# Attention and gated feed-forward on one core: first transfers in another order, sinks' product with 64 weight columns, late values products reordered

## The chip, the cores and the metric

The kernel runs on one core of a Trainium2 chip. The core has five engines that run side by side: TensorE (PE, with its weight loads shown apart as PEld), VectorE (DVE), ScalarE (ACT), GpSimd (POOL) and SyncE (SP), which here only issues transfers. ACT issues a few transfers too. Each engine takes its instructions strictly in the order of its list and waits at an instruction until what it needs is there. The metric is the device time of one execution in microseconds (us); of several runs the median is given.

## The reference, cut to what matters

Attention with a window of 128 positions and a few sink positions that every row may see, for 4 batches of 8 heads, 768 positions and 64 dimensions per head; its output, with heads side by side as 512 columns, goes through a gated feed-forward layer.

```python
scores = scale * np.matmul(q, k.transpose(0, 1, 3, 2))
is_sink = pos[None, :] < int(n_sink)
rel = pos[:, None] - pos[None, :]
in_window = (rel >= 0) & (rel < int(window))
scores = np.where(is_sink | in_window, scores, -1000000000.0)
a = softmax(scores)
attn = np.matmul(a, v)                      # (4, 8, 768, 64)
x = attn.transpose(0, 2, 1, 3).reshape(3072, 512)
h = x @ w_in                                # (3072, 2048)
g = h * np.cos(h)
out = g @ w_out                             # (3072, 512)
```

## The kernel before

**Tiling.** Queries are worked in chunks of 256 rows (CB = 2 blocks of 128). The first four chunks are the first 256 rows of the four batches ("early" chunks, which have no sink columns of their own); then follow, batch by batch, two "late" chunks (rows 256 and 512). Two chunks make a pair of 512 columns for the feed-forward layer: `h_pair` (L476) and `out_pair` (L521) run 12 and 12 products of 512 columns per slice of 128 hidden units, in fp32r with operands split into a high and a low part. While the feed-forward of one pair runs on PE, the attention of the next pair is woven between its products.

**What sets the order.** A planner (`Plan.order`) simulates five engines with estimated durations and due times and gives one list of steps; each step appends its instructions to the list of one engine. The engines then keep to these lists. A step's function may issue more instructions than its planned duration says; the planner looks at the duration alone.

**Start.** `setup` runs before the planned steps. On ACT it issues the two limits `n_sink` and `window` (L235, L236) and the first two weight pieces `raw_70` and `raw_71` (L247, 512 KB each). SP begins with the planned loads of the first q pair (`xq`, L923, two transfers of 64 KB) and the first k pair (`xk`). The limits are spread over 128 partitions by a small product on PE (L266, `both`) and make the masks on DVE (L1538 to L1563). Between the masks DVE converts the 64-bit weights of `raw_70` and `raw_71` (three instructions each, L583, L589, L595). The first softmax instruction of DVE is L1046. Idle products (L1532) stand on PE's list between the first real ones. `xq` and `xk` are single buffers: SP's next load of q waits until PE has turned the last one (L931). Transfers share eight completion semaphores in turn, so a transfer also waits until the eighth before it has landed.

**Late chunks.** Per head, `values` (L1215) makes seven products into one bank `av`: the two blocks of 128 keys at the edge give one product of 128 columns each for the high (weights 128 columns wide: high and low values side by side) and low probabilities (64 weight columns), the middle block one of 256 columns each, and one of 256 columns is the sinks' product, whose weights are `x1r` (the sinks' values) and whose moving operand is `gt`. `gt` comes from `sink_cols` (L1105, L1107 on DVE: for four heads the eight sink columns of p, rounded and rest, side by side in `gc`), a transpose on PE (L1120) and a copy. `x1r` is made once per batch by `vs_part` (L1095, L1096, four times two instructions on DVE) from `yt`, which `load_batch_v` (L858) fills with eight small transfers on SP, also once per batch. The first batch's eight are on SP's list early, behind the third weight piece; those of the others come at 292, 404 and 516 us.

The order of the products in `values` before:

```python
seq = [wide_hi]
if o.sj:
    seq.append((o.av[:, o.sj[0] * P :], lhs, gt[:, : len(o.sj) * P]))
seq += [*narrow[:2], wide_lo, *narrow[2:]]
```

## Time and profile before

| | |
|---|---|
| median of 3 runs | 726.91 us (726.79 to 726.95) |
| profiled execution, first to last instruction | 725.6 us |
| PE busy | 708.8 us (98%) |
| PEld / DVE / ACT / POOL busy | 584.1 / 599.3 / 527.7 / 127.5 us |
| transfers | 77.13 MB, mean 106 GB/s |
| granted TensorE clock | 0.999 of full speed |

The profiled execution is given by its span, 725.6 us; what lies around the span brings it to the time of the runs, 1.3 us more. The page's busy shares are means over stages: until about 70 us the early attention runs with ACT and DVE nearly full and idle products on PE; from 70 to 700 us PE is busy almost without a gap; the last 26 us store the output and check the inputs' range. A row of the timeline reads: start, duration, engine, line, operation, output<-inputs, size, count, and in brackets the idle time before it with what ended it. SPq and ACTq rows are transfers being issued; the time is that of the issue, not of the landing.

### The profile page before, as it was taken

To read this page: it belongs to the slowest core of one execution; us is meant where nothing else is said; L and a number is where in the kernel's file an instruction comes from. 1 tells how busy PE (TensorE), PEld (TensorE's weight loads), DVE (VectorE), ACT (ScalarE), POOL (GpSimd) and SP (SyncE) were. 2 spreads that over 40 slices of the span, in tenths; PEclk is the share of its full clock that TensorE was granted. 3 is DMA by queue.
4 is the path that set the end of the run, shared out by engine and by line. 5 is a ranking of instruction groups with operands and counts; after the bars stand their busy time and mean duration, and the time that the engine had idled before them with its cause. 6 is when DMAs were issued, how large, how long until landed. Compare 5 with 4: busy or idle time off the path is not lost.

```text
span 725.6 us, 12986 instructions
## 1 busy us (share of the span) xinstructions
PE 708.8 (98%) x3674; PEld 584.1 (81%) x3674; DVE 599.3 (83%) x1849; ACT 527.7 (73%) x1344; POOL 127.5 (18%) x213
## 2 busy tenths in 40 slices
PE   7998999999999999999999999999999999999996
PEld 7766787888888888888888888888888888888884
DVE  6889998988988978988978988878989865667762
ACT  3896976788697697796686886776887766566642
POOL 1010000001223222232231222232123222100000
PEclk9999999999999999999999999999999999999999
DMA  5665555533256333355433254433254500375551
GB/s 144 182 186 153 158 162 162 141 65 68 68 118 146 73 62 57 72 119 124 93 60 59 56 131 103 118 61 64 43 139 99 119 18 12 97 210 148 164 137 64
DMA packets 236501, 77.13 MB, mean 106 GB/s; under 512 B 221060, under 2 KB 221060, under 8 KB 236420
## 3 DMA queue, kind: packets, MB, share of 16 engines
q1 hardware_dynamic: 236128, 75.15, 43.4%
q10 hardware_dynamic: 292, 1.05, 0.5%
q8 instruction: 32, 0.52, 0.3%
q14 instruction: 49, 0.40, 0.2%
HBM read 69.86 MB, written 6.29 MB: 105 GB/s over the span
## 4 chain that ended last, share of the span: by engine, by line
PE 81%; ACT 11%; DVE 4%; issue 2%; DMA 1%; SPq 0%; ACTq 0%; DVEq 0%
PE acc L521 32%; PE h L476 32%; PE av L1215 5%; PE s L1024 4%; ACT p L1055 3%; PE s L968 2%; PE av L1191 2%; PE tp L1136 2%; ACT p L1073 1%; PE tp L1146 1%; PE qk L931 1%; ACT L485 1%; PE idle L1532 1%; ACT L1055 1%; ACT early L390 1%
## 5 line engine op out<-in xcount | busy, mean ns | idle before, releaser
L521 PE MATMUL acc<-whi_out,ghi 128*128 128x512 f32 x384 | 161.8, 421 | 0.0
L476 PE MATMUL h<-xhi,whi_in 128*128 128x512 f32 x384 | 155.2, 404 | 0.0
L476 PE MATMUL h<-xlo,whi_in 128*128 128x512 f32 x384 | 150.9, 393 | 0.0
L521 PE MATMUL acc<-whi_out,glo 128*128 128x512 f32 x384 | 150.8, 393 | 0.0
L521 PE MATMUL acc<-wlo_out,ghi 128*128 128x512 f32 x384 | 150.1, 391 | 0.0
L476 PE MATMUL h<-xhi,wlo_in 128*128 128x512 f32 x384 | 150.0, 391 | 0.0
L1174 POOL TENSOR_SCALAR_AFFINE_SELECT ph<-ph 128x512 fp32r<-128x512 f32 x128 | 87.4, 683 | 230.3 <-DVE ph L1167 226.4
L485 ACT ACTIVATE r<-h 128x512 f32<-128x512 f32 x96 | 57.1, 598 | 48.6 <-PE h L476 46.0
L476 PEld LDWEIGHTS h<-xlo,whi_in 128*128 128x128 f32 x384 | 72.1, 188 | 16.3
L521 PEld LDWEIGHTS acc<-whi_out,glo 128*128 128x128 f32 x384 | 72.1, 188 | 16.2
L476 PEld LDWEIGHTS h<-xhi,whi_in 128*128 128x128 f32 x384 | 72.2, 188 | 12.0 <-DVE r L498 0.3
L476 PEld LDWEIGHTS h<-xhi,wlo_in 128*128 128x128 f32 x384 | 72.4, 189 | 11.2
L521 PEld LDWEIGHTS acc<-whi_out,ghi 128*128 128x128 f32 x384 | 72.8, 190 | 10.7
L521 PEld LDWEIGHTS acc<-wlo_out,ghi 128*128 128x128 f32 x384 | 72.7, 189 | 9.4
L1055 ACT ACTIVATE p<-p,st 128x136 f32<-128x136 f32 (+1 forms) x192 | 79.2, 416 | 0.3
L498 DVE SCALAR_TENSOR_TENSOR r<-r,h 128x512 f32<-128x512 f32 x96 | 64.6, 674 | 16.9 <-ACT r L491 16.1
L506 ACT CAST ghi<-r 128x512 fp32r<-128x512 f32 x96 | 59.5, 619 | 22.8 <-PE acc L521 15.7
L512 DVE TENSOR_TENSOR glo<-r,ghi 128x512 fp32r<-128x512 f32 x96 | 66.3, 691 | 7.1 <-ACT ghi L506 6.3
L1046 DVE CUSTOM_DVE_ANT_0 p<-s,mk 128x136 f32<-128x136 f32 (+1 forms) x192 | 59.8, 313 | 6.5 <-PE s L968 3.1
L984 ACT CAST l<-tq 64x256 fp32r<-64x256 f32 x64 | 25.8, 403 | 46.7 <-PE s L1024 46.4
L1032 DVE COPY_PREDICATED s<-mk,s 128x128 f32<-128x128 int32 x128 | 37.3, 291 | 24.6 <-PE s L1024 22.5
L1024 PEld LDWEIGHTS s<-r,l 128*128 128x128 f32 x256 | 46.5, 188 | 12.3 <-DVE ph L1167 1.5
(153 smaller groups left out, 1302.3 us busy)
## 6 DMA issues: line engine op xcount, KB each, us to landing
xk<-in_k_dram SPq DMA_DIRECT2D x256, 48.0 KB
raw<-in_moe_w_out_dram SPq DMA_DIRECT2D x16, 512.0 KB
wt<-in_moe_w_in_dram SPq DMA_DIRECT2D x32, 256.0 KB
raw<-in_moe_w_in_dram SPq DMA_DIRECT2D x14, 512.0 KB
v<-in_v_dram SPq DMA_DIRECT2D x64, 96.0 KB
raw<-in_v_dram SPq DMA_DIRECT2D x32, 192.0 KB
out_dram<-wt SPq DMA_DIRECT2D x22, 256.0 KB
wt<-in_moe_w_out_dram SPq DMA_DIRECT2D x20, 256.0 KB
```

Source lines behind the costliest of these rows:

```text
L476: nc.tensor.matmul(out=o.h, lhsT=w[:, c, fs], rhs=xx[:, c, :], start=(c == 0 and n == 0), stop=(c == NC - 1 and n == 2),)
L485: nc.scalar.activation(out=o.r, in_=o.h, func=AF.Sin, scale=0.5)
L498: nc.vector.scalar_tensor_tensor(out=o.r, in0=o.r, scalar=0.5, in1=o.h, op0=ALU.subtract, op1=ALU.mult)
L506: nc.scalar.copy(out=o.ghi, in_=o.r)
L512: e.tensor_tensor(out=o.glo, in0=o.r, in1=f32(o.ghi), op=ALU.subtract)
L521: nc.tensor.matmul(out=y.acc[j], lhsT=gg[:, j * P : (j + 1) * P], rhs=w[:, f, :], start=(f == 0 and n == 0), stop=(f == NFT - 1 and n == 2),)
L1024: nc.tensor.matmul(out=o.s_ps[j][:, :w], lhsT=o.l[:, j * P : (j + 1) * P], rhs=r.rearrange("p n s -> p (n s)")[:, c0 : c0 + w], start=(n = ...
L1032: nc.vector.copy_predicated(out=o.s_ps[j][:, :P], mask=below.bitcast(I32), data=o.s_ps[j][:, SW : SW + P])
L1046: nc.vector.tensor_tensor_reduce(out=o.pj[j][:, :w], in0=o.s_ps[j][:, :w], in1=masks[min(o.i0 + j, 2)][:, :w], op0=ALU.add, op1=ALU.min, s ...
L1055: nc.scalar.activation(out=o.pj[j][:, :w], in_=o.pj[j][:, :w], func=AF.Exp, bias=o.lead.st[:, 0, o.nth, j : j + 1], scale=-1.0, accum_out= ...
L1174: nc.gpsimd.affine_select(out=ph[:, :, b, :], in_=f32(ph)[:, :, 1, :], pattern=[[0, 2 * CB], [(-1, 1)[b], P]], compare_op=(ALU.is_gt, ALU. ...
L1215: nc.tensor.matmul(out=dst, lhsT=lhs, rhs=rhs, start=(n == 0), stop=(n == len(seq) - 1), skip_group_check=True)
```

## The change

The change does four things.

1. **First transfers.** The planned steps for the first q and k loads no longer issue them; `setup` does, first of all: q on SP, k on ACT. The limits go to SP behind q, `raw_70` to ACT behind k, and `raw_71` to SP behind the limits.
2. **Sinks' values.** `load_batch_v` issues 16 small transfers per batch in place of 8 (each group of 8 sink rows four times). `vs_part` runs three instructions in place of two, on 32 partitions in place of 16: it rounds the values, multiplies by a column `odd16` that is -1 on every second group of 8 partitions and 0 else, and adds the values. High and low values so stand below each other on partitions and not side by side in columns. `x1r` has 512 columns to blank in place of 1024. `odd16` is made at the start by one POOL and two DVE instructions.
3. **Sink columns.** `sink_cols` writes the rounded part and the rest twice (32 elements per partition and instruction in place of 16), `gc` has 128 columns for each block in place of 112, its transpose and the copy to `gt` 128 partitions in place of 112. The sinks' product has 64 weight columns.
4. **Order of the products in `values`.** First block high and low, sinks, third block high and low, middle block low, middle block high.

```diff
-        nc.scalar.dma_start(out=nw_i[:, 0, :], in_=n_sink.unsqueeze(0))
-        nc.scalar.dma_start(out=nw_i[:, 1, :], in_=window.unsqueeze(0))
+        for e, load in zip((nc.sync, nc.scalar), env.boot):
+            load(e)
+        nc.sync.dma_start(out=nw_i[:, 0, :], in_=n_sink.unsqueeze(0))
+        nc.sync.dma_start(out=nw_i[:, 1, :], in_=window.unsqueeze(0))
...
+        nc.gpsimd.iota(odd16.bitcast(I32), pattern=[[0, 1]], base=0, channel_multiplier=1)
...
-        for raw, src in env.first:
-            nc.scalar.dma_start(out=raw.rearrange("p n w -> p (n w)"), in_=src)
+        for e, (raw, src) in zip((nc.scalar, nc.sync), env.first):
+            e.dma_start(out=raw.rearrange("p n w -> p (n w)"), in_=src)
...
-                    for dup in range(2):
+                    for dup in range(4):
...
+        def booting(load):
+            env.boot.append(load)
+
+            def fn(e):
+                pass
+            return fn
...
-                w = sink_values().rearrange("p (g a) b c d -> p g (a b) c d", g=2)
-                r = slice(h * 32, h * 32 + 2 * NSINK)
-                e.tensor_copy(out=w[r, :, h, 0, :], in_=o.vs32[r])
-                e.tensor_tensor(
-                    out=w[r, :, h, 1, :], in0=o.vs32[r], in1=f32(w)[r, :, h, 0, :], op=ALU.subtract
-                )
+                r = slice(h * 32, h * 32 + 32)
+                w = sink_values()[r, :, h // 2, h % 2, :]
+                e.tensor_copy(out=w, in_=o.vs32[r])
+                e.tensor_scalar(out=w, in0=f32(w), scalar1=odd16[r], scalar2=1.0, op0=ALU.mult, op1=ALU.mult)
+                e.tensor_tensor(out=w, in0=f32(w), in1=o.vs32[r], op=ALU.add)
...
+                        out=g5.bitcast(F32R)[:, :, h, :, 0],
+                        in_=oo.p[:, :, P:SW].unsqueeze(2).broadcast_to([P, CB, 2, NSINK]),
...
-                seq = [wide_hi]
-                if o.sj:
-                    lhs = sink_values()[:, o.pair, o.odd].rearrange("p a d -> p (a d)")
-                    seq.append((o.av[:, o.sj[0] * P :], lhs, gt[:, : len(o.sj) * P]))
-                seq += [*narrow[:2], wide_lo, *narrow[2:]]
+                sinks = o.av[:D], sink_values()[:, o.h // 4, o.pair % 2, o.odd], gt
+                seq = [
+                    block(0, o.phi, 2 * D), block(0, o.plo, D), sinks, block(2, o.phi, 2 * D),
+                    block(2, o.plo, D), block(1, o.plo, D), block(1, o.phi, 2 * D),
+                ]
...
-                    i = add(dma(2), load_natural(xq_t, src, CB), [bx], pq, lat=2.3 if g else 1.9)
+                    load = load_natural(xq_t, src, CB)
+                    i = add(dma(2), load if g else booting(load), [bx], pq, lat=2.3 if g else 1.9)
```

The planner's estimates are the same, and no step changes its place among the others. What changes on the lists is shown at three places.

SP's list from its first transfer, before (`xq` and `xk` are a pair's q and k, `vpe` and `v_76` values of the early chunks, `yt` the sinks' values of the first batch):

```order
L923 DMA xq<-in_q_dram 128x2x64 x2
L923 DMA xk<-in_k_dram 128x2x64 x2
L904 DMA vpe<-in_v_dram 128x2x64
L904 DMA v_76<-in_v_dram 128x2x64
L923 DMA xq<-in_q_dram 128x2x64 x2
L923 DMA xk<-in_k_dram 128x2x64 x2
L568 DMA raw_70<-in_moe_w_in_dram 128x1024
L858 DMA yt<-in_v_dram 8x2x64 x8
L923 DMA xq<-in_q_dram 128x2x64 x2
```

It was q, k, values, the second pair, the third weight piece, eight sink loads and then the third pair's q. The same place with the change:

```order
L930 DMA xq<-in_q_dram 128x2x64 x2
L236 DMA nw_i<-in_n_sink_dram 1x2
L237 DMA nw_i<-in_window_dram 1x2
L249 DMA raw_71<-in_moe_w_in_dram 128x1024
L911 DMA vpe<-in_v_dram 128x2x64
L911 DMA v_76<-in_v_dram 128x2x64
L930 DMA xq<-in_q_dram 128x2x64 x2
L930 DMA xk<-in_k_dram 128x2x64 x2
L575 DMA raw_70<-in_moe_w_in_dram 128x1024
L865 DMA yt<-in_v_dram 8x2x64 x16
L930 DMA xq<-in_q_dram 128x2x64 x2
```

The first k has left SP's list for ACT's, limits and `raw_71` have come to it, and the third pair's q stands behind 16 sink loads.

PE's list at one late head, the first of the second batch, before (`av` is the head's output bank, `ph` the probabilities, `vr` its values, `gt` and `x1r` the sinks):

```order
L1215 MATMUL av_2_0_3657<-ph_2_0_3588,vr_2_0_3524 128x256
L1215 MATMUL av_2_0_3657<-gt,x1r 128x256
L1215 MATMUL av_2_0_3657<-ph_2_0_3588,vr_2_0_3524 128x128
L1215 MATMUL av_2_0_3657<-ph_2_0_3588,vr_2_0_3524 64x128
L1215 MATMUL av_2_0_3657<-ph_2_0_3588,vr_2_0_3524 64x256
L1215 MATMUL av_2_0_3657<-ph_2_0_3588,vr_2_0_3524 128x128
L1215 MATMUL av_2_0_3657<-ph_2_0_3588,vr_2_0_3524 64x128
L521 MATMUL acc_0_2335<-whi_out,ghi_3566 128x512
```

The feed-forward product (L521) follows two products of 128 columns. With the change:

```order
L1228 MATMUL av_2_0_3684<-ph_2_0_3611,vr_2_0_3539 128x128
L1228 MATMUL av_2_0_3684<-ph_2_0_3611,vr_2_0_3539 64x128
L1228 MATMUL av_2_0_3684<-gt,x1r 64x256
L1228 MATMUL av_2_0_3684<-ph_2_0_3611,vr_2_0_3539 128x128
L1228 MATMUL av_2_0_3684<-ph_2_0_3611,vr_2_0_3539 64x128
L1228 MATMUL av_2_0_3684<-ph_2_0_3611,vr_2_0_3539 64x256
L1228 MATMUL av_2_0_3684<-ph_2_0_3611,vr_2_0_3539 128x256
L528 MATMUL acc_0_2350<-whi_out,ghi_3589 128x512
```

Now it follows the product of 256 columns; the sinks' product is third and not second. All 64 late heads have these two orders.

DVE's list where the first batch's sink values are made, before:

```order
L1095 CAST x1r<-yt 16x2x64
L1096 TENSOR_TENSOR x1r<-yt,x1r 16x2x64
L1095 CAST x1r<-yt 16x2x64
L1096 TENSOR_TENSOR x1r<-yt,x1r 16x2x64
L1095 CAST x1r<-yt 16x2x64
L1096 TENSOR_TENSOR x1r<-yt,x1r 16x2x64
L1095 CAST x1r<-yt 16x2x64
L1096 TENSOR_TENSOR x1r<-yt,x1r 16x2x64
```

These are four parts of two instructions each. With the change:

```order
L1109 CAST x1r<-yt 32x2x64
L1110 TENSOR_SCALAR x1r<-x1r,neg 32x2x64
L1111 TENSOR_TENSOR x1r<-x1r,yt 32x2x64
L1109 CAST x1r<-yt 32x2x64
L1110 TENSOR_SCALAR x1r<-x1r,neg 32x2x64
L1111 TENSOR_TENSOR x1r<-x1r,yt 32x2x64
```

Each of the four parts has one instruction more (two of the four are shown), on the same number of elements per partition.

## Rows read from the trace of the kernel before

**Rows 1.** The page: span, and busy time of each engine
```profile
span 725.6 us, 12986 instructions
PE 708.8 (98%) x3674; PEld 584.1 (81%) x3674; DVE 599.3 (83%) x1849; ACT 527.7 (73%) x1344; POOL 127.5 (18%) x213
```
**Rows 2.** Stretches: us, busy by engine (instructions), granted clock, transfers' share, GB/s
```profile
30.00:40.00 10.00, 9.12 (x56) 7.22 (x55) 9.14 (x34) 9.63 (x34) 0.00 (x0) 1.00 0.69 180
...
300.00:400.00 100.00, 99.69 (x541) 83.17 (x540) 85.85 (x280) 77.49 (x200) 27.30 (x45) 1.00 0.42 91
```
**Rows 3.** Timeline of PE around the values products of one late head
```profile
300.39 0.40 PE L521 MATMUL acc<-whi_out,glo 128*128 128x512 f32 x1
300.62 0.28 PE L1215 MATMUL av<-ph,vr 128*128 128x256 f32 x1
300.74 0.28 PE L1215 MATMUL av<-gt,x1r 128*128 128x256 f32 x1
300.87 0.53 PE L1215 MATMUL av<-ph,vr 128*128 128x128 f32 x5
301.23 0.45 PE L521 MATMUL acc<-whi_out,ghi 128*128 128x512 f32 x1
301.51 0.40 PE L521 MATMUL acc<-wlo_out,ghi 128*128 128x512 f32 x1
```
**Rows 4.** Timeline of the start, all engines
```profile
1.38 0.22 ACTq L236 DMA_DIRECT2D nw_i<-in_window_dram  x1
...
1.63 1.54 ACTq L247 DMA_DIRECT2D raw<-in_moe_w_in_dram  x2
...
2.96 0.16 DVE L265 CAST sm<-nw_i 1x4 f32<-1x4 int32 x1 [0.19 <-DMA nw_i<-in_window_dram]
...
4.47 0.16 DVE L269 COPY neg<-both 128x2 f32<-128x2 f32 x1 [1.35 <-PE both L266]
...
6.39 0.43 DVE L583 TENSOR_SCALAR wt<-raw 128x512 int32<-128x512 int32 x1 [0.72 <-DMA raw<-in_moe_w_in_dram]
...
7.69 0.66 PE L931 MATMUL qk<-ident,xk 128*128 128x128 f32 x2 [2.10 <-DMA xk<-in_k_dram]
...
9.83 0.34 SPq L568 DMA_DIRECT2D raw<-in_moe_w_in_dram  x1
...
10.27 3.74 SPq L858 DMA_DIRECT2D yt<-in_v_dram  x8
...
10.78 0.28 DVE L1046 CUSTOM_DVE_ANT_0 p<-s,mk 128x128 f32<-128x128 f32 x1
...
14.53 0.91 SPq L923 DMA_DIRECT2D xq<-in_q_dram  x2
...
18.54 0.38 PE L931 MATMUL qk<-ident,xq 128*128 128x128 f32 x2
...
20.02 0.37 ACT L390 COPY early<-qk 64x256 f32<-64x256 f32 x1 [3.30 <-PE qk L931]
```
**Rows 5.** Waits of SP's queue: line, releaser: us in total, times, longest
```profile
SPq L858 <- DMA raw<-in_moe_w_in_dram: 1.1, 1, 1.1
```
**Rows 6.** Timeline of DVE where the second batch's sink values are made
```profile
296.59 0.66 DVE L1095 CAST x1r<-yt 16x128 fp32r<-16x128 f32 x1
...
299.92 0.23 DVE L1095 CAST x1r<-yt 16x128 fp32r<-16x128 f32 x1
300.18 0.29 DVE L1096 TENSOR_TENSOR x1r<-yt,x1r 16x128 fp32r<-16x128 f32 x1
```
**Rows 7.** Timeline of DVE and PE at the first batch's sinks
```profile
187.50 0.29 DVE L1096 TENSOR_TENSOR x1r<-yt,x1r 16x128 fp32r<-16x128 f32 x1
...
188.75 0.28 PE L1215 MATMUL av<-gt,x1r 128*128 128x256 f32 x1
```
**Rows 8.** Stretches of 1 us at the start, columns as in rows 2
```profile
7.00:8.00 1.00, 0.31 (x2) 0.34 (x3) 0.90 (x5) 0.00 (x0) 0.00 (x0) 1.00 0.93 232
8.00:9.00 1.00, 1.00 (x6) 1.00 (x5) 0.97 (x5) 0.61 (x2) 0.00 (x0) 1.00 0.17 37
```

More of the change, by code (lines that the diff above doesn't have):

```diff
@@ L19 @@
 SW = P + NSINK
-GR = 96 + 2 * NSINK
 BW = 2 * P + NSINK
@@ L256, in setup @@
         nc.vector.tensor_copy(out=rc, in_=rc_i)
+        nc.vector.tensor_scalar(
+            out=odd16.bitcast(I32), in0=odd16.bitcast(I32), scalar1=4, scalar2=1,
+            op0=ALU.logical_shift_right, op1=ALU.bitwise_and,
+        )
+        nc.vector.tensor_single_scalar(out=odd16, in_=odd16.bitcast(I32), scalar=-1.0, op=ALU.mult)
         nc.vector.tensor_single_scalar(out=env.below, in_=rel, scalar=0.0, op=ALU.is_lt)
@@ L833, in x1r @@
                 env.x1r = ap.tile([P, NP * NT], F32R, name="x1r", tag="x1")
-                env.vs = env.x1r.rearrange("p (a b c d) -> p a b c d", a=NP, b=2, c=2)
+                env.vs = env.x1r[:, : NP * 2 * D].rearrange("p (g a o d) -> p g a o d", g=2, o=2, d=D)
             return env.x1r
@@ L922, in fn @@
                 for h in range(2):
-                    nc.sync.dma_start(out=dst[:, :, h, :], in_=src(h).rearrange("(n s) d -> s n d", s=P))
+                    e.dma_start(out=dst[:, :, h, :], in_=src(h).rearrange("(n s) d -> s n d", s=P))
+            return fn
[3 more added lines that the diff above has]
+                pass
             return fn
@@ L1117, in fn @@
             def fn(e):
-                o.gp = late_bank(o, 2)[:GR]
-                for n, j in enumerate(o.sj):
-                    nc.tensor.transpose(
-                        out=o.gp[:, n * P : (n + 1) * P], in_=gc[:, j], identity=ident,
-                    )
+                o.gp = late_bank(o, 2)
+                for j in range(CB):
+                    nc.tensor.transpose(out=o.gp[:, j * P : (j + 1) * P], in_=gc[:, j], identity=ident)
             return fn
@@ L1126, in fn @@
             def fn(e):
-                w = len(o.sj) * P
-                copy(e, gt[:GR, :w], o.gp[:, :w])
+                copy(e, gt, o.gp)
             return fn
@@ L1200, in fn, with block @@
                 o.av = late_bank(o, 1)
-                mms = {}
-                for t, w in ((o.phi, 2 * D), (o.plo, D)):
-                    for n, (kb, qs) in enumerate(o.cols):
-                        dst = o.av[:w, (qs[0] - o.i0) * P : (qs[-1] + 1 - o.i0) * P]
-                        lhs = o.vr[:, kb - o.kb0].rearrange("p a d -> p (a d)")[:, :w]
-                        mms.setdefault((w, len(qs)), []).append((dst, lhs, t[:, o.offs[n] * P : o.offs[n + 1] * P]))
-                (wide_hi,), (wide_lo,) = mms[2 * D, CB], mms[D, CB]
-                narrow = [m for pair in zip(mms[2 * D, 1], mms[D, 1]) for m in pair]
-                seq = [wide_hi]
-                if o.sj:
-                    lhs = sink_values()[:, o.pair, o.odd].rearrange("p a d -> p (a d)")
-                    seq.append((o.av[:, o.sj[0] * P :], lhs, gt[:, : len(o.sj) * P]))
-                seq += [*narrow[:2], wide_lo, *narrow[2:]]
+                def block(n, t, w):
+                    kb, qs = o.cols[n]
+                    return (
+                        o.av[:w, (qs[0] - o.i0) * P : (qs[-1] + 1 - o.i0) * P],
+                        o.vr[:, n].rearrange("p a d -> p (a d)")[:, :w], t[:, o.offs[n] * P : o.offs[n + 1] * P],
+                    )
+                sinks = o.av[:D], sink_values()[:, o.h // 4, o.pair % 2, o.odd], gt
[3 more added lines that the diff above has]
+                ]
                 for n, (dst, lhs, rhs) in enumerate(seq):
@@ L1237, in x_sum @@
             return fn
-        env.first = []
+        env.first, env.boot = [], []
         early = [buf("plo", 1), buf("vr", 1), buf("v32", C["XV"])]
@@ L1337, in before_softmax @@
                     pk = t - 7 * T + C["DQ"] + 1.2 if g else C["LD"] - 1
-                    i = add(dma(2), load_natural(xk_t, src, o.nkb), [bx], pk, lat=2.4 if g else 1.9)
+                    load = load_natural(xk_t, src, o.nkb)
+                    i = add(dma(2), load if g else booting(load), [bx], pk, lat=2.4 if g else 1.9)
                     i = add(
```

13 lines of the change are left out of this document (7 added, 6 removed).

## The prediction, made before the changed kernel was run

> **What bounds the kernel now.** I read the page first, then busy time by stretches, then the timelines of three places: a late head, the making of the sinks' values, and the start. The page shows PE busy for 708.8 of 725.6 us [rows 1]; the question is which stages make up the rest and what an edit is worth in each. Between 300 and 400 us PE is busy for 99.69 of 100 us, while DVE and ACT have room [rows 2]: there, whatever PE no longer does, and whatever it has to wait for, goes to the end almost in full. Between 30 and 40 us ACT is busy for 9.63 and DVE for 9.14 of 10 us [rows 2], and PE's share is high only because idle products stand on its list. Engines keep to their lists, so a delay that reaches ACT and DVE before 30 us is not worked off; it reaches the end too. The granted clock is 1.00 in these rows (2.4 GHz, the upper of its two levels), and nothing in the change empties PE for longer than before, so I leave it there. The profiled execution spans 725.6 us, the median run is 726.91; the 1.3 us between them I take over unchanged. So three sums are wanted: products' order (all late heads), start (once), sinks' values (once per batch).
>
> **Order of the products: -2.8 us.** PE's starts are the measure, since the ends of pipelined products overlap. A feed-forward product of 512 columns moves the next start on by 0.23 us (300.39 to 300.62) [rows 3]. The two of 256 columns take 0.12 and 0.13, the five that follow 0.36 together, that is four of 0.06 and one of 0.12. But the first feed-forward product after them takes 0.28 (301.23 to 301.51), 0.05 more than its kin [rows 3]. It is the one whose full weights (128 columns) must be loaded while a product of only 128 columns (0.06 us) runs; I read the 0.05 as the part of that load that stands out. After the change it follows a product of 256 columns, twice the cover, and 0.05 is less than the 0.06 that this adds. The seven products are the same in kind and columns (the sinks' weights are half as wide, which the steps do not show to matter: wide and narrow weights alike step by 0.06). 64 late heads times 0.05 is 3.2 us. About 0.3 us in 100 are idle on PE [rows 2], that is, in some places PE waits for others already, and there the gain only makes it wait longer; for this I take off 0.4. Bounds: 0 (the 0.05 is something else) and -3.3.
>
> The Trainium skill, page "TensorE: Matmul & The Clock Gate", section "The mechanism", says that a weight load overlaps running products only when it goes to another group of rows of the array. Taken alone that would put every load of 128 rows on the path and make the reorder worth nothing. The trace does not agree: weight loads and products together are busy for 584.1 + 708.8 us in a span of 725.6 [rows 1].
>
> **Start: +1.5 us.** What goes: PE waits 2.10 us for the first k until 7.69 [rows 4]. That wait ends earlier. But what is late next is on DVE: its first softmax instruction (10.78) stands behind its list of masks and weight pieces, and that list stood still for 0.72 us until `raw_70` had landed at 6.39 [rows 4]. From there to 10.78 are 4.39 us of list that do not shrink. So k alone is worth nothing unless `raw_70` is early; call d the shift of 6.39.
>
> The limits: the cast at 2.96 comes 1.58 us after the second limit's issue at 1.38 [rows 4]. Behind q's two issues (0.91 as at 14.53 [rows 4]) this is 3.9. Now 1.35 us of DVE's wait until 4.47 are for PE's small product behind warm-up products, so of the 0.9 I let a third remain (an estimate), and DVE reaches `raw_70`'s first instruction not at 6.39 - 0.72 = 5.67 but near 6.0. That gives d = -0.4 as the lower bound. `raw_70` itself: it is issued at about the time as before (two q-sized issues of k in place of the limits), k's 128 KB ahead of it. `raw_71`, though, no longer stands behind it on one queue but on SP's, in flight beside it. Transfers move 232 GB/s from 7 to 8 us and 37 from 8 to 9 [rows 8], so the first burst ends near 8.2; a weight piece (512 KB) takes 2.3 us alone at that rate. Served one after the other, `raw_70` lands about where it did, k's 0.57 us against the bytes of k and v that no longer mix with it: d near 0. Shared by halves, with `raw_71` issued 0.4 to 0.8 us behind (the limits' two issues, 0.22 or more each [rows 4]), `raw_70` lands that much before 8.3: d = 1.1 to 1.5. Landing together is the upper end, d = 1.9. I take 1.0, next to sharing.
>
> d goes on through SP: the third weight piece (9.83) needs `raw_70`'s buffer and moves by d [rows 4]. Behind it eight sink loads took 3.74 us, of which 1.1 were one wait for that piece to land [rows 4, 5]: (3.74 - 1.1) / 8 = 0.33 each. Sixteen take 2.65 more, so they end not at 14.01 but at 16.7 + d. The third pair's q, issued from 14.53 to 15.44, now goes from 16.7 + d; its second half is issued at 17.15 + d and needs 1.6 us (the limits' time) to 2.0, landing near 18.75 to 19.2 + d. PE turns it at 18.54, and ACT at 20.02 has already sat idle for 3.30 for PE's turns [rows 4], so ACT is moved by what PE is: +0.2 to +0.7, taken 0.5, plus d. Sum 1.5; bounds 0.1 (d = -0.4) and 2.4 (d = 1.9).
>
> **Sinks' values: +2.5 us.** Each part has one instruction more. In the second batch a part's first instruction takes 0.26 to the next (299.92 to 300.18) [rows 6]; the new one has the same 128 elements per partition, so four are 1.0 us on DVE, which runs these parts without a gap. One may be stretched as the first is (0.66 us [rows 6]): then 1.4. `sink_cols` has 16 elements more in each of eight instructions, too few for any row to price; up to 0.2. The last instruction now ends at 300.18 + 0.29 = 300.47 and the product that reads it starts at 300.74 [rows 3, 6]: of the 0.27 some 0.1 go to the weight load and the hand-over, so about 0.2 is slack and 0.8 becomes a wait of PE, behind which the whole feed-forward queues. Two of the narrow products now stand ahead of the sinks' in place of the wide one, 0.12 either way, so this does not move. Three batches of such a kind are 2.4. The first batch's last instruction ends at 187.50 + 0.29 = 187.79, its product starts at 188.75 [rows 7]: 0.96 of slack, 0.1 left. Together 2.5. Bounds 0.5 (DVE finds room ahead of the parts, as it is 85.85% busy there [rows 2]) and 3.9 (1.4 less 0.1 of slack, three times).
>
> At no cost: eight more loads per batch on SP later, 2.65 us, hidden behind the four heads that lie between their issue and their use (if not, the wait would show at the same product); 16 more partitions in the sinks' transposes and copies; two DVE and one POOL instruction at the start, which fall into the 1.35 and 0.72 that DVE waits there [rows 4].
>
> **Sum.** -2.8 + 1.5 + 2.5 = +1.2; 725.6 + 1.2 + 1.3 = 728.1 us. Its own range, with d from 0.2 to 1.5 and the sinks from 1.8 to 3.2, is 726.9 to 729.3.
>
> **Rivals.**
> B, faster: `raw_70` is on time and the sinks' values are covered. d = -0.4 gives 0.1 at the start, the sinks cost 0.5 and the order gives all of 3.2: -2.6, 724.3 us. For it: DVE has 14% of room in the late stages [rows 2]. Against: in the row where it counts the parts follow each other without a gap, 0.27 before their use [rows 3, 6].
> C, slower: the two weight pieces on two queues are served in turns and land together near 8.3. Then d = 1.9, the start costs 2.4, the sum is +2.1: 729.0 us. It decides from d = 1.25 on, since there the sum passes +1.45. For it: DVE waited for this very transfer, and the burst has no spare rate [rows 4, 8]. Against: `raw_70` is issued first and has a lead. The Trainium skill, page "DMA: Bandwidth & Descriptors", section "Queues, rings and completion order", says that each transfer engine goes round the queues that have work, a packet from each; that would be this rival. No row of before has two weight pieces on two queues.
> D, slower, the order does nothing: the 0.05 us after the values is not a weight load, but comes with the change from values to feed-forward, whatever the last columns are. Then 1.5 + 2.5 = +4.0: 730.9 us. For it: within the values 128-column products step by 0.06 with weights of 128 columns too, and nothing stands out there [rows 3]. Against: full loads hide wherever at least 256 columns run ahead of them, and only the cover is shorter here.
>
> **Chances.** Forecast 0.46, B 0.20, C 0.18, D 0.10, other 0.06. A measurement of this kernel can tell 0.2%, 1.45 us, from no change: 725.46 to 728.36 is "same". The forecast's own range puts 0.33 there and 0.13 above; B is faster; C and D are slower; of the rest 0.02, 0.03 and 0.01. So faster 0.22, same 0.36, slower 0.42. The range of 724.9 to 730.0 leaves out half of B, most of D and little else.
>
> **What would show it.** Right: DVE's L590, first on `raw_70`, later than 6.39 by about 1; SP's sink loads ending near 17.7 and the third pair's q turned by PE near 20.0; feed-forward products after the values stepping by 0.23; PE idle 0.8 us in the second, third and fourth batch before the first product that reads `x1r`. Wrong: L590 on time (B), the first product after the values still at 0.28 (D), or no wait before `x1r`'s reader. If the start's delay is there but ACT and DVE are caught up at 70 us, my claim that a delay of the early stage reaches the end is wrong.

## The result, and the profile after

The changed kernel takes 733.76 us (median of 4 runs, 733.05 to 734.57), the kernel before 726.93 on the same chip: a ratio of 1.0095, interval 1.0083 to 1.0107, or +6.9 us. The forecast was +1.2 (728.1, with a range to 730.0): right in sign, far off in size. The profiled execution is the shortest of the four, 733.05 us with a span of 731.3, so its own sum (5.7 us over [rows 1]) is 0.7 short of the median's, and 1.7 lie around it where 1.3 were taken over.

The page: span, and busy time of each engine.

```profile
span 731.3 us, 13064 instructions
PE 708.5 (97%) x3674; PEld 578.4 (79%) x3674; DVE 605.1 (83%) x1867; ACT 528.5 (72%) x1344; POOL 127.5 (17%) x214
```

PE is busy for as long as before [rows 1] and idle for longer. The same stretch in the middle of a batch in both shows it, first before, then after.

```profile
305.00:400.00 95.00, 94.69 (x513) 79.01 (x512) 81.03 (x267) 73.40 (x190) 26.30 (x43) 1.00 0.43 92
```

```profile
305.00:400.00 95.00, 93.81 (x509) 77.17 (x509) 81.75 (x269) 71.81 (x189) 25.97 (x43) 1.00 0.44 96
```

Granted clock 1.00 in both; PE's idle time has grown from 0.31 to 1.19 us in 95.

**Where it came in.** Each trace has the same 2304 products of 512 columns on PE. The start of the n-th in one trace less its start in the trace of before shows when a kernel falls behind (us; the head gives the time in the trace of before):

| kernel | 56 | 188 | 192 | 293 | 320 | 405 | 416 | 518 | 530 | 712 |
|---|---|---|---|---|---|---|---|---|---|---|
| changed | 2.86 | 2.40 | 3.23 | 3.10 | 4.24 | 4.00 | 5.27 | 5.04 | 6.28 | 6.18 |
| fused | 3.26 | 2.92 | 2.87 | 2.63 | 3.21 | 3.10 | 3.16 | 3.08 | 3.44 | 3.42 |
| order_only | 0.85 | 0.76 | 0.76 | 0.88 | 0.94 | 1.10 | 1.15 | 1.29 | 1.34 | 1.28 |
| before16 | 2.18 | 2.10 | 2.10 | 2.08 | 2.57 | 2.59 | 2.61 | 2.72 | 2.99 | 2.89 |
| before_gc | 0.49 | 0.07 | 0.02 | 0.29 | 0.31 | 0.53 | 0.59 | 0.76 | 0.83 | 1.12 |

The changed kernel is late after the start, falls back at the first head of each of the four batches (0.8, 1.1, 1.3 and 1.2 us), and in between wins back no more than 0.1 to 0.25 where the order should give 0.8 in 16 heads. Part of what is missing there is a drift of 0.2 to 0.3 us per batch that the wider sink columns alone show too (before_gc). Order_only has the start of before, unchanged, and yet 0.85 at 56: a single execution's start is known to no better than that. Taken together, and read in the same way for the other runs, the starts still part: three kernels with the start of before (order_only, before_gc, before_vpool) are 0.5 to 0.9 late at 56, four with sixteen loads and otherwise that start (before16, sinks_only, sinks_order, late_fused) 1.9 to 2.9. Fused had a granted clock of 0.50 from 21.0 to 24.4 us, so its start is not the change's alone.

**The start**, all engines, answering [rows 4] and [rows 5].

```profile
2.22 0.23 SPq L237 DMA_DIRECT2D nw_i<-in_window_dram  x1
...
5.50 0.16 DVE L272 CAST sm<-nw_i 1x4 f32<-1x4 int32 x1 [3.00 <-DMA nw_i<-in_window_dram]
...
7.45 0.42 DVE L590 TENSOR_SCALAR wt<-raw 128x512 int32<-128x512 int32 x1
...
11.32 6.52 SPq L865 DMA_DIRECT2D yt<-in_v_dram  x16
...
17.94 0.90 SPq L930 DMA_DIRECT2D xq<-in_q_dram  x2
...
20.49 0.41 PE L945 MATMUL qk<-ident,xq 128*128 128x128 f32 x2 [2.07 <-DMA xq<-in_q_dram]
...
22.00 0.37 ACT L397 COPY early<-qk 64x256 f32<-64x256 f32 x1 [5.55 <-PE qk L945]
```

The wait for k is gone (PE turns it at 7.25 without one). The limits, forecast for 3.9, are cast at 5.50, 3.3 us after their issue where it was 1.58: beside q, k and the weight pieces even eight bytes come late. `raw_70` is begun at 7.45 without a wait for it, so d (the shift of that first instruction on `raw_70`, before at 6.39) is 1.06, close to the 1.0 that was taken, but set by the limits. The sink loads end at 17.84, and PE turns the third pair's q at 20.49, 1.95 later than before.

**A late head**, PE, answering [rows 3].

```profile
303.79 0.39 PE L528 MATMUL acc<-whi_out,glo 128*128 128x512 f32 x1
304.02 0.28 PE L1228 MATMUL av<-ph,vr 128*128 128x128 f32 x2
304.14 0.28 PE L1228 MATMUL av<-gt,x1r 128*64 128x256 f32 x1
304.26 0.51 PE L1228 MATMUL av<-ph,vr 128*128 128x128 f32 x4
304.61 0.39 PE L528 MATMUL acc<-whi_out,ghi 128*128 128x512 f32 x1
304.84 0.39 PE L528 MATMUL acc<-wlo_out,ghi 128*128 128x512 f32 x1
305.07 0.40 PE L528 MATMUL acc<-whi_out,glo 128*128 128x512 f32 x1
306.09 0.41 PE L1149 MATMUL tp<-ident,p 128*128 128x128 f32 x2 [0.62 <-DVE st L1060]
```

The product after the values now steps by 0.23 (304.61 to 304.84): the 0.05 is saved, as forecast. But there is no wait before the product that reads `x1r`, where the forecast had it; PE waits 1.5 us later, at the transpose for a softmax that DVE is late with.

**The sinks' values of the second batch**, last part, DVE, answering [rows 6].

```profile
303.96 0.23 DVE L1109 CAST x1r<-yt 32x128 fp32r<-32x128 f32 x1
304.22 0.28 DVE L1110 TENSOR_SCALAR x1r<-x1r,neg 32x128 fp32r<-32x128 f32 x1
304.54 0.29 DVE L1111 TENSOR_TENSOR x1r<-x1r,yt 32x128 fp32r<-32x128 f32 x1
```

This part ends at 304.83, yet the sinks' product of the batch's first head began at 304.14: it needs its own part alone, the first, which had ended at 301.42.

### The profile page after: what moved, and what is told of

It reads as the page before. It is cut to its first block, busy times and chain, and to the rows that moved or that the text cites. A ratio compares the mean times of both kernels' runs of the same rounds, so it can differ in the third digit from the quotient of the medians.

```text
span 731.3 us, 13064 instructions
## 1 busy us (share of the span) xinstructions
PE 708.5 (97%) x3674; PEld 578.4 (79%) x3674; DVE 605.1 (83%) x1867; ACT 528.5 (72%) x1344; POOL 127.5 (17%) x214
## 4 chain that ended last, share of the span: by engine, by line
PE 71%; ACT 11%; DVE 10%; DMA 3%; issue 3%; SPq 1%; DVEq 0%; ACTq 0%
PE h L483 28%; PE acc L528 27%; PE av L1228 4%; PE s L1038 3%; ACT p L1069 3%; PE av L1204 2%; PE s L982 2%; PE tp L1149 2%; DMA xq<-in_q_dram 2%; ACT p L1087 1%; DVE glo L519 1%; PE tp L1159 1%; ACT L492 1%; PE qk L945 1%; ACT early L397 1%
## 5 line engine op out<-in xcount | busy, mean ns | idle before, releaser
L528 PE MATMUL acc<-whi_out,ghi 128*128 128x512 f32 x384 | 160.0, 417 | 0.0
```

The costliest lines, as they stand in the source:

```text
L528: nc.tensor.matmul(out=y.acc[j], lhsT=gg[:, j * P : (j + 1) * P], rhs=w[:, f, :], start=(f == 0 and n == 0), stop=(f == NFT - 1 and n == 2),)
```

## The experiments

Ratios are to the kernel before, timed beside each on the same chip. Microseconds are medians. Where a difference between two of these kernels is called good to so many us, that is half of its 95% interval, worked out from the two ratios.

**order_only.** The kernel before with the new order; sinks' weights stay 128 columns.

```diff
-                seq = [wide_hi]
-                if o.sj: ...
-                seq += [*narrow[:2], wide_lo, *narrow[2:]]
+                seq = [*narrow[:2], sinks, *narrow[2:], wide_lo, wide_hi]
```

> The kernel before with only the late values products in the new order (the sinks' product keeps 128 weight columns). Theory A (the gain is eaten): the step after the values falls from 0.28 to 0.23 us in all 64 heads, 3.3 us on PE, but PE then waits longer at the few places where it already waits for the softmax on DVE (0.3 to 0.4 us at 327, 375, 406 us and their like in each batch), so less than 1.5 us reach the end: 725.4 to 726.9 us. Theory B (the gain was lost only because the sinks' values slow DVE): alone the order gives 2.5 to 3.3 us, 723.6 to 724.4 us.

727.23 us, 1.0004 (0.9995 to 1.0013): no change. Neither theory had the reason. PE around the values:

```profile
301.50 0.28 PE L1213 MATMUL av<-ph,vr 128*128 128x128 f32 x2
301.62 0.33 PE L1213 MATMUL av<-gt,x1r 128*128 128x256 f32 x1
301.79 0.53 PE L1213 MATMUL av<-ph,vr 128*128 128x128 f32 x4
302.16 0.39 PE L521 MATMUL acc<-whi_out,ghi 128*128 128x512 f32 x1
302.39 0.40 PE L521 MATMUL acc<-wlo_out,ghi 128*128 128x512 f32 x1
```

The 0.05 has moved: the feed-forward product steps by 0.23, but the sinks' takes 0.17 (301.62 to 301.79) where it took 0.13 [rows 3]. Its full weights now stand behind a product of 128 columns. With 64 weight columns it steps by 0.12 in the changed kernel. So the order needs the narrow sinks' weights; the forecast had called their width indifferent.

**start_only.** The kernel before with the first transfers of the change alone.

```diff
+        for e, load in zip((nc.sync, nc.scalar), env.boot):
+            load(e)
+        nc.sync.dma_start(out=nw_i[:, 0, :], in_=n_sink.unsqueeze(0))
...
+        for e, (raw, src) in zip((nc.scalar, nc.sync), env.first):
```

> The kernel before with only the first transfers in the new order (eight sink loads per batch as before). Theory A (limits and sink loads both count): the limits are cast near 5.5 us and the first weight piece is begun near 7.45 as in the changed kernel, but the third pair's q is issued near 15.5 and not 17.9, so PE turns it at 18.6 to 19.3 us (18.54 before, 20.49 changed) and the end moves by +0.5 to +1.2: 727.4 to 728.1 us. Theory B (the late limits are all of it): +2.4 to +2.9, 729.3 to 729.8 us. Theory C (the sixteen loads are all of it): 726.6 to 727.2 us.

728.04 us, 1.0010 (1.0001 to 1.0019): theory A in its time, +0.7 to +1.0. Here DVE did wait for the weight piece:

```profile
7.18 0.43 DVE L585 TENSOR_SCALAR wt<-raw 128x512 int32<-128x512 int32 x1 [0.37 <-DMA raw<-in_moe_w_in_dram]
```

PE turned the third pair's q at 19.53, outside theory A's 18.6 to 19.3, but without a wait for it. In this execution PE had been idle for 1.93 us until 12.00, and the granted clock was 0.57 from 12 to 16 us; the ten others show a mean clock of 0.997 to 0.999 where this one has 0.995. So the 19.53 says nothing of when that q came.

**sinks_only.** The changed kernel with first transfers and order as before.

```diff
-        for e, load in zip((nc.sync, nc.scalar), env.boot):
-            load(e)
...
+                    block(1, o.phi, 2 * D), sinks, block(0, o.phi, 2 * D), block(0, o.plo, D),
+                    block(1, o.plo, D), block(2, o.phi, 2 * D), block(2, o.plo, D),
```

> The kernel before with only the sinks' part of the change: sixteen loads per batch, three DVE instructions per part, 64 weight columns; products and first transfers stand as before. Theory A (the third DVE instruction, once per batch, delays the softmax behind it and PE waits there): a jump of 0.8 to 1.1 us on PE at each of 189, 301, 413 and 525 us, together about 4, and from the sixteen loads at the start 0.3 to 1.2: 731.2 to 732.1 us. Theory B (the jumps came from PE arriving earlier through the new order, not from DVE): below 729.5 us.

734.41 us, 1.0103 (1.0088 to 1.0118), +7.5: more than the whole change, and more than theory A had. The sixteen loads of the start are in it, which the forecast had counted with the start.

**fused.** The changed kernel with two instructions per part:

```diff
-                e.tensor_scalar(out=w, in0=f32(w), scalar1=odd16[r], scalar2=1.0, op0=ALU.mult, op1=ALU.mult)
-                e.tensor_tensor(out=w, in0=f32(w), in1=o.vs32[r], op=ALU.add)
+                e.scalar_tensor_tensor(out=w, in0=f32(w), scalar=odd16[r], in1=o.vs32[r], op0=ALU.mult, op1=ALU.add)
```

> The changed kernel with multiplication and addition of the sinks' values in one DVE instruction: two per part, as before the change, all else as changed. Theory A (the number of DVE instructions makes the jumps): the jumps at 189, 301, 413 and 525 us fall from 0.85 to 1.1 to below 0.3 us each, the time by 3 to 4 us: 729.8 to 730.8 us. Theory B (wider sink columns, sixteen loads or the late order make them): 732.8 to 734.6 us, as the changed kernel.

730.22 us, 1.0044 (1.0030 to 1.0058), 3.7 below the changed kernel by the ratios (good to 1.3). Theory A in its time; the steps at the batches shrink to -0.05, 0.58, 0.06 and 0.36 (table), two of them not below the 0.3 that it had.

**limits_first.** The changed kernel with the limits back in front on ACT.

```diff
+        nc.scalar.dma_start(out=nw_i[:, 0, :], in_=n_sink.unsqueeze(0))
+        nc.scalar.dma_start(out=nw_i[:, 1, :], in_=window.unsqueeze(0))
         for e, load in zip((nc.sync, nc.scalar), env.boot):
             load(e)
-        nc.sync.dma_start(out=nw_i[:, 0, :], in_=n_sink.unsqueeze(0))
-        nc.sync.dma_start(out=nw_i[:, 1, :], in_=window.unsqueeze(0))
```

> The changed kernel with the two limits where they were, first on ACT's queue, k and the first weight piece behind them; SP's queue begins with q and the second weight piece. Theory A (limits behind q and beside k cast at 5.5 us move the masks, the first weight piece and the third by 1 us): the cast is back near 3.0 to 3.5 us, the third pair's q is turned about 1 us earlier than 20.49, and the time falls by 0.6 to 1.5 us from the changed kernel, 732.3 to 733.2 us. Theory B (the first weight piece, sharing with the second, sets the start, not the limits): 733.4 to 734.2 us, and DVE waits for the piece.

734.54 us, 1.0112 (1.0097 to 1.0127): not better, theory A fails in its number; DVE waits for the piece, as theory B had it. But this kernel changed more than meant, as its start shows.

```profile
1.82 0.46 SPq L249 DMA_DIRECT2D raw<-in_moe_w_in_dram  x1
...
2.60 0.49 ACTq L249 DMA_DIRECT2D raw<-in_moe_w_in_dram  x1
...
2.72 0.20 DVE L272 CAST sm<-nw_i 1x4 f32<-1x4 int32 x1 [0.21 <-DMA nw_i<-in_window_dram]
...
8.22 0.43 DVE L590 TENSOR_SCALAR wt<-raw 128x512 int32<-128x512 int32 x1 [2.54 <-DMA raw<-in_moe_w_in_dram]
```

The limits come early (2.72), but without them on SP `raw_71` is issued 0.8 us before `raw_70` and is served first: it is there at 6.3, `raw_70` at 8.2, and DVE waits 2.54 us. In the changed kernel `raw_70` has the lead and is there at 7.1, `raw_71` at 8.4. So limits and piece are late by much the same, and moving one leaves the other. Rival C's landing together is not what happens: the earlier issue lands clearly earlier.

**late_fused.** Fused, with the first transfers as before the change.

> First transfers as before the change; sixteen loads, 64 weight columns, the late order, and two DVE instructions per part. Theory A (the sixteen loads early on SP still cost 0.8 to 1.1 us, and the order's 3.3 us of PE are mostly eaten by waits for DVE's softmax): 727.3 to 728.6 us. Theory B (order gains in full once its sinks' weights are 64 columns wide and DVE is not burdened): 724.3 to 725.5 us.

728.95 us, 1.0032 (1.0020 to 1.0045): just above theory A's range, far from B. In the second batch DVE waits for k, which SP issued behind the sixteen loads:

```profile
306.14 0.58 DVE L1009 STREAM_TRANSPOSE tk<-xk 128x384 f32<-128x384 f32 x1 [0.79 <-DMA xk<-in_k_dram]
```

**best_fused** and **best_pool.** The first batch's loads moved to the first late `load_v`; in best_pool the parts also on POOL.

```diff
+                if env.later is None:
+                    env.later = loads
+                    return
...
+                e = nc.gpsimd
```

> As late_fused, but the first batch's sixteen loads are issued at about 172 us, with the first values of the late chunks, and not at 10 us. Theory A (sixteen loads ahead of the third pair's q are the rest of the start's delay): 0.7 to 1.3 us below late_fused; by the waits for DVE 726.3 to 727.5 us. Theory B (the loads are not on the path): the same as late_fused.

> As best_fused, but the sinks' values are made on POOL (three instructions per part), so that DVE has 2.2 us less in each batch than before the change. Theory A (the order's gain is held back by DVE's list, which lags PE): the jumps on PE at 189, 301, 413 and 525 us turn into gains of 0.5 to 1 us each, 723.5 to 725.5 us. Theory B (another chain than DVE's list holds the gain back, or POOL is late for the first product that reads the values): 726.3 us or more.

731.35 us (1.0059, 1.0046 to 1.0072) and 731.79 (1.0068, 1.0049 to 1.0087): both worse than late_fused, because the new place was bad. SP's queue in best_fused, and PE's wait behind it:

```profile
172.21 5.47 SPq L869 DMA_DIRECT2D yt<-in_v_dram  x16
177.78 0.93 SPq L918 DMA_DIRECT2D v<-in_v_dram  x2
```

```profile
181.67 0.48 PE L1155 MATMUL tp<-ident,p 128*128 128x128 f32 x1 [3.15 <-ACT p L1094]
```

By the products' starts this cost 4.6 us between 172 and 180, after a start that was not late. Of these, 3.7 are there at 178, with the wait; 0.9 come in the 2 us after it, when the granted clock was 0.51 (181.67 to 184.50 in best_fused) and products of 512 columns stepped by 0.43 in place of 0.23. After 192 best_pool's shift stays between 4.2 and 5.5 to the end: DVE's relief alone, beside that late place, did not let the order's gain out, so theory A of best_pool falls.

**loads8, loads8_old, loads8_drop, loads8_vpool.** Late_fused with eight loads that read their rows four times; then with the old order; with one product per head left out (so a part of each head's result is missing); and with the values rounded on POOL.

```diff
+                        in_=rows[:, n].unsqueeze(0).broadcast_to([4, NSINK, D])
...
-                    block(2, o.plo, D), block(1, o.plo, D), block(1, o.phi, 2 * D),
+                    block(1, o.plo, D), block(1, o.phi, 2 * D),
...
-                nc.scalar.copy(out=o.vr[:, :, 0, :], in_=o.v32)
+                nc.gpsimd.tensor_copy(out=o.vr[:, :, 0, :], in_=o.v32)
```

> First transfers as before the change, late order, 64 weight columns, two DVE instructions per part as in late_fused; but a batch's sinks' values come in eight transfers, each of 32 partitions that reads its eight rows four times, and not in sixteen. Theory A (the sixteen issues on SP are what is left: they push the third pair's q at the start and in the second batch k, for which DVE waited 0.79 us at 306): 1 to 2 us below late_fused, 726.7 to 727.9 us. Theory B (number of issues does not matter): 728.5 to 729.5 us.

> As loads8, with the seven products in the order of before the change (middle block, sinks, edges). The pair with loads8 measures the order by itself. Theory A (PE's 3.3 us are eaten at the three places in each chunk where PE waits for the lists of ACT and DVE): equal to loads8 within 1 us. Theory B (PE sets the pace and the order was hidden by the other parts): 2.5 to 3.3 us above loads8.

> As loads8, with one product of 128 columns per late head left out (third block with the low probabilities): 64 times 0.06 us less on PE, 3.8 us, and nothing less on ACT or DVE. Theory A: PE's waits grow instead, less than 1.3 us reach the end. Theory B: 3.3 to 3.8 us below loads8.

> As loads8, with the rounding of the values (128x192, 0.35 us per late head on ACT) on POOL instead of ACT; PE and DVE have the same instructions. Theory A (ACT's list, full without a gap for 8 us ahead of PE's waits though ACT is busy for only 77% of the late stage, holds PE back): PE's waits shrink and the time falls by 0.5 to 3 us from loads8. Theory B (PE sets the pace, or POOL is late with the values): the same or more.

loads8: 728.94 us, 1.0024 (1.0015 to 1.0033), as late_fused; theory B by the median. Fewer issues did not help; SP was held nearly as long by eight wide ones:

```profile
10.05 5.55 SPq L863 DMA_DIRECT2D yt<-in_v_dram  x8
```

loads8_old: 730.58, 1.0049 (1.0035 to 1.0063): the order is worth 1.6 to 1.8 us (good to 1.2) of the 3.3 that were to be had, between the theories. loads8_drop: 729.94, 1.0043 (1.0029 to 1.0056): 3.8 us less on PE and not faster. loads8_vpool: 726.91, 0.9998 (0.9989 to 1.0006): 2.0 us faster, with nothing taken from PE or DVE. Theory A in both. PE's waits at the transposes of the softmax (`tp`) between 70 and 625 us (in total, times, longest) in loads8 and in loads8_vpool; PE's other waits there sum to 1.8 and 1.6 us:

```profile
PE tp L1146 <- DVE st L1058: 0.8, 4, 0.2
PE tp L1146 <- ACT p L1085: 0.7, 3, 0.2
```

```profile
PE tp L1146 <- DVE p L1087: 0.2, 1, 0.2
```

What stands ahead of such a wait is seen in the chain of waits of the kernel before, in one chunk:

```profile
254.39 0.61 PE av L1215 x7
...
255.29 0.35 ACT vr L1083
...
258.16 1.08 ACT p L1055 x5
...
262.55 0.37 ACT yt L1222
262.92 0.25 ACT vr L1083
263.17 0.32 ACT p L1073
263.53 0.33 PE tp L1136
```

For 8 us the chain runs through ACT's list alone, and PE's transpose at its end is released by ACT. ACT is busy for 77% of the late stage [rows 2], but for 8.08 of the 8.21 us from 255.29 to 263.50. The rounded values (`vr`) themselves come in time wherever they are made: in before, before_vpool, loads8 and loads8_vpool they are complete more than 2.1 us before a head's first product, in all 64 heads. So it is ACT's room that counts here, not an earlier landing of the values.

**loads8_old_vpool.** Loads8_vpool with the old order.

> As loads8_vpool, with the seven products in the order of before the change. Theory A (ACT's list is what keeps part of the order's gain from the end): with ACT relieved the order is worth more than the 1.6 us it is worth without that, 2.2 to 3.3 us, so this kernel is at 1.0030 to 1.0045 of the kernel before, where loads8_vpool is at 0.9998. Theory B (other waits keep it): 1.0022 or less.

729.57 us, 1.0044 (1.0032 to 1.0057), against 0.9998: 0.0046, or 3.3 us (good to 1.1). Theory A. By the ratios alone 3.3 and the 1.8 without ACT's relief do not part clearly; the traces bear it out. From the products at 56 to those at 712 us (times of before) the order shortens the vpool pair by 3.0 us and the loads8 pair by 1.0 (table in the next section).

**before16.** The kernel before with twice the loads, so that partitions are filled which nothing reads.

```diff
-                    for dup in range(2):
+                    for dup in range(4):
```

> The kernel before with sixteen loads per batch in place of eight (the eight more fill partitions that nothing reads); nothing else is changed. Theory A (the loads hold up the third pair's q at the start and k in the second batch): +1.2 to +2.5 us from the kernel before, some of it by 30 us and a jump of 0.4 to 0.8 between 300 and 320 us. Theory B (hidden, as predicted): less than 0.6 us.

730.58 us, 1.0052 (1.0039 to 1.0066), +3.4 to +3.8: above theory A. SP's queue and PE at the start, and SP's queue in the second batch:

```profile
10.01 6.54 SPq L858 DMA_DIRECT2D yt<-in_v_dram  x16
16.65 0.91 SPq L923 DMA_DIRECT2D xq<-in_q_dram  x2
...
293.93 5.70 SPq L858 DMA_DIRECT2D yt<-in_v_dram  x16
```

```profile
19.21 0.41 PE L931 MATMUL qk<-ident,xq 128*128 128x128 f32 x2 [1.36 <-DMA xq<-in_q_dram]
...
25.05 0.41 PE L931 MATMUL qk<-ident,xq 128*128 128x128 f32 x2 [1.11 <-DMA xq<-in_q_dram]
```

PE waits not once but twice: the fourth pair's q is late as well. The second wait is not the sixteen loads' alone: in loads8_old, with eight wide ones, it is 1.54 us, in loads8, with the same start, 0.30.

**before_gc.** The kernel before with the wider sink columns alone.

```diff
-GR = 96 + 2 * NSINK
+GR = 128
...
+                        out=g5.bitcast(F32R)[:, :, h, :, 0],
+                        in_=oo.p[:, :, P:SW].unsqueeze(2).broadcast_to([P, CB, 2, NSINK]),
```

> The kernel before with the wider sink columns alone: 32 elements per partition and instruction in place of 16, transposes and copies of 128 partitions in place of 112. The eight added rows per head meet rows of the sinks' weights that are zero. Theory A (the wide columns delay DVE ahead of the sinks' transpose, for which PE waits): +0.5 to +1.5 us, in steps of 0.1 to 0.2 at the four transposes of each batch. Theory B: less than 0.4 us.

728.54 us, 1.0021 (1.0011 to 1.0030), +1.4: theory A, though it comes as a slow drift over each batch (table) and less in steps. The instruction that takes the rest of the sink columns (duration in ns, least, median, most), before and changed:

```profile
L1107 DVE TENSOR_TENSOR gc<-p,gc x64: 161/168/177, 181.9 to 602.2; 128x16 f32<-128x16 f32 x64
```

```profile
L1123 DVE TENSOR_TENSOR gc<-p,gc x64: 180/185/191, 184.4 to 608.5; 128x32 f32<-128x32 f32 x64
```

**sinks_order.** The changed kernel with the first transfers as before (the first two lines of the edit of sinks_only, with the order left as changed).

> The changed kernel with the first transfers as before the change: sixteen loads, three DVE instructions per part and the late order stay. If the parts add up, it is 1.0 to 1.3 us below the changed kernel (what the start costs by start_only and by fused against late_fused), 732.4 to 732.9 us, and 1.5 to 2.0 us below sinks_only (what the order gives). If the start and the sixteen loads get in each other's way, it is 2 us or more below the changed kernel, at 731.8 us or less.

732.98 us, 1.0077 (1.0063 to 1.0091): 0.8 us below the changed kernel by the medians (1.3 by the ratios, good to 1.3) and 1.4 (1.9, good to 1.5) below sinks_only. By the ratios both are where they had to be if the parts add up, by the medians a little below; intervals of this width show no more than that nothing large is hidden between start and loads.

**before_vpool.** The kernel before with the rounding of the values on POOL, the last line of the diff above.

> The kernel before with the rounding of the late values on POOL instead of ACT, nothing else. Theory A (ACT's list holds PE back in the kernel before as well): 1 to 2.5 us faster, 724.6 to 726.1 us. Theory B (the kernel before is paced by PE alone, as the prediction had it): within 0.5 us.

726.04 us, 0.9982 (0.9973 to 0.9991), against 727.17 for the kernel before beside it: theory A, at the small end. It is the one version here whose interval lies below the kernel before. The instruction itself costs POOL what it cost ACT, before and here:

```profile
L1083 ACT CAST vr<-v x64: 347/351/355, 176.0 to 615.8; 128x192 fp32r<-128x192 f32 x64
```

```profile
L1083 POOL CAST vr<-v x64: 343/347/818, 174.6 to 615.0; 128x192 fp32r<-128x192 f32 x64
```

## Why the prediction was wrong, point by point

By the ratios the three parts measure +7.5 (sinks_only), -1.9 (sinks_order against it) and +1.3 (the changed kernel against sinks_order): +6.9. They are three steps of one path, so that they add up proves nothing, and each is good to 1.1 to 1.5 us. The forecast had +2.5, -2.8 and +1.5, or, with the sixteen loads of the start counted with the sinks as in sinks_only, +3.0, -2.8 and +1.0. The step that failed is the sinks' values, first of all their loads.

- **"At no cost: eight more loads per batch on SP", and "taken 0.5" for those of the start.** The step that failed most. Alone the loads cost 3.4 to 3.8 us (before16), where the sum had 0.5. Most of it is at the start: of the 2.9 us that before16's trace is late at the end, 2.2 are there at 56 us, and against the three kernels with the start of before the four with sixteen loads are 1.0 to 2.4 late there. The forecast had set their 2.65 us of issue against one pair's q; in before16 the next pair's q is late too. Later the loads cost another 0.8 (2.10 at 188, 2.89 at 712), where the forecast had nothing: in the second batch 0.5, and there DVE waits 0.4 us for k. Four heads between issue and use were taken as cover for the sink loads themselves; what was not asked is which other transfers stand behind them on SP, in that same batch.
- **"16 more partitions in the sinks' transposes and copies" at no cost, `sink_cols` up to 0.2 us.** 1.4 us (before_gc). The widening of one instruction is 0.017 us at the median. It is not longer waiting: PE's idle time does not grow, its busy time does, by 1.1 us (table below). How 64 such instructions come to that stays open.
- **The third instruction per part.** Forecast 2.4 us as waits before the product that reads `x1r` in three batches; measured 3.7 (fused, good to 1.3). The mechanism was wrong in its place: each head's product needs its own part, not all four, so PE does not wait there. The whole of the added time (four steps of 0.31 us) delays what stands behind on DVE, and PE waits for that: in the second batch for the softmax, in the first for a feed-forward operand (`glo`, 0.46 us at 192.71). And so the first batch, with its 0.96 us of slack before `x1r` [rows 7], pays like the others (0.8 in the table). The three costs sum to 8.7, above the 7.5 of sinks_only; the intervals allow that, and whether they share waits is not shown.
- **The order.** The 0.05 us was a weight load, and it is gone in all 64 heads (0.28 to 0.23); with the values' own steps PE saves 0.047 per head, 3.0 us. Rival D fell. It was the claim on the bound that failed: "whatever PE no longer does goes to the end almost in full". Taking 3.8 us more from PE brought nothing (loads8_drop), taking 0.35 us per head from ACT brought 2.0 (loads8_vpool). An engine busy for 99.7% of a stretch was not the only one that set its length. The forecast took off 0.4 for places where PE waits already; between loads8_old and loads8 the idle time alone grows by 1.6.
- **The start's transfers.** The change of 1.0 that was taken for them was close: 0.7 alone, 1.3 in company. The size of d was right by luck: the limits were to be cast at 3.9 and were at 5.50, and it was they, with no wait for `raw_70` at 7.45, that set it; in start_only it was the piece, at 7.18. The start as a whole, loads included, is 2.86 late at 56, or 2.0 to 2.4 against the three kernels above; the sum had 1.5.
- **Rival C** gave 729.0 for a landing together that did not occur; rival B's premise, sinks covered by DVE's room, is the opposite of what happened.

That a delay of the start reaches the end was right: of 2.86 us at 56, 2.40 were left at 188, before the first late head.

PE from the products at 56 to those at 712 us (times of before), in us:

| kernel | length | busy | idle |
|---|---|---|---|
| before | 656.11 | 652.76 | 3.35 |
| changed | 659.43 | 652.93 | 6.50 |
| sinks_only | 661.09 | 655.90 | 5.19 |
| before_gc | 656.75 | 653.85 | 2.90 |
| loads8_old | 657.85 | 654.28 | 3.57 |
| loads8 | 656.86 | 651.71 | 5.15 |
| loads8_drop | 656.52 | 649.03 | 7.49 |
| loads8_old_vpool | 657.25 | 653.75 | 3.50 |
| loads8_vpool | 654.26 | 650.43 | 3.83 |

What PE no longer does turns into idle time in loads8 (from loads8_old: busy -2.6, idle +1.6) and still more in loads8_drop (-2.7, +2.3), and goes to the end with ACT relieved (loads8_vpool from loads8_old_vpool: -3.3, +0.3). The table also shows a cost that no sum had: the sinks' part makes PE busy for 3.1 us longer (sinks_only), which the order takes back. About 1.0 of it is a step: in the old order with 64-column sink weights the values and the first feed-forward product take 0.891 us per head where they took 0.875. The rest is not located; busy time also holds waits too short to show between overlapping products, as loads8_vpool has the same products as loads8 and 1.3 us less of it.

## What to carry to other kernels

An engine busy for nearly all of a stretch is a bound only between the places where it waits: follow the chain of waits through each of those few places, since there another engine's list, full for some microseconds, can take back what the first one saves. For work added to a queue or an engine, ask not whether its own result is in time but which instructions and transfers stand behind it, in every stage where it recurs. Test a term by taking away the supposed bound's work: if the time stays, the sum had the wrong engine.

## What the runs showed of the hardware

A full weight load (128 columns) stands out by 0.05 us behind a product of 128 columns and not behind one of 256, whatever comes next: in the kernel before at the feed-forward product, in order_only at the sinks' product. A load of 64 columns stands out behind neither. The Trainium skill, page "TensorE: Matmul & The Clock Gate", section "The mechanism", says in one place that a weight load overlaps running products only in another group of rows, and in another that it may also go ahead into a background weight buffer. The traces bear out the second: steps of 0.06 and 0.12 us leave no room for loads of all 128 rows that wait for products of all 128 rows.

A transfer of a few bytes issued at 2.22 us beside 256 KB of q and k and the weight pieces was there 3.3 us later, against 1.58 in the kernel before, where q alone had been issued ahead of it. Eight sink loads of 32 partitions held SP's queue for 5.55 us with no wait among them, eight of 8 partitions for 3.74 [rows 4] and sixteen of these for 6.54 (before16), the last two with a wait of 1.1 each: 0.6 us per wide load, 0.3 per narrow one.

The granted clock fell to the lower of its two levels (1.2 GHz) behind stretches in which PE stood idle: in best_fused after 3.15 us of waiting (0.51 from 181.67 to 184.50), in the profiled start_only after 1.93 us (0.57 from 12 to 16). It did not fall at the wait of 2.07 us until 20.49 in the changed kernel (1.00 there).
